# Windowed attention ahead of a mixture of experts: scores issued before the neighbouring unit's transposes, four shared PSUM banks

## The chip, the cores and the metric

The kernel runs on one core of a Trainium2 chip. The core has five engines with queues of their own: TensorE (PE; its weight loads are shown as PEld), VectorE (DVE), ScalarE (ACT), GpSimd (POOL) and SyncE (SP), which here issues the transfers. Matmul results go to PSUM, which has eight banks, each of 512 fp32 per partition. The metric is the device time of one execution in microseconds (us), given as the median of several runs; smaller is better.

## What is computed

Three stages, one after the other: attention with a causal window of 64, a mixture of experts with a greedy assignment under a capacity, and a two-layer network.

```python
B, H, S, D = 4, 8, 576, 64
scores = q @ k.T / 8, kept where 0 <= i - j < 64, otherwise -1e9
attn = exp(scores - rowmax); attn = attn / (attn.sum(-1) + 1e-9)
x = (attn @ v) laid out as [B*S, H*D]            # 2304 tokens of 512
logits = x @ w_gate                              # 8 experts
# greedy: largest logit first, at most 288 tokens per expert, one expert per token
x = relu(x @ w1[e]) @ w2[e]                      # e: the token's expert
h = relu(x @ w_in);  out = (h * h) @ w_out
```

## The kernel before, in words

`attention` comes first and fills some 130 us; then the routing, whose counting needs the logits of all tokens, and the two feed-forward stages follow. Their program is the same in both kernels. The routing starts from the last logits that `attention` writes to `L`.

**Units.** The attention's work is cut into 18 units. Unit 3n+j stands for a batch pair and a block of 64 rows: n (0 to 5) is a pair of batches (n even: batches 0 and 1, n odd: 2 and 3) in a third of the sequence (n//2), j is the block in that third. A unit has two batches times 64 rows on 128 partitions, and eight heads. Four pieces of work belong to a unit:

- `scores(u)`: 32 small matmuls into the tile `sp` (two banks, one buffer; line 130); then eight times on VectorE the mask, scale and row minimum (L135, the tiles t and mn) and on ScalarE the exponential (L136) into P.
- `ptr_(u)`: P is transposed by TensorE in two halves of four transposes (L142), each half into a bank named pt, and each copied to PT by ScalarE (L143).
- `pv(u)`: 32 matmuls of PT with the window of v (L154) into `po` (two banks, one buffer), then on VectorE den (L157), the reciprocal (L159) and X, the product (L160). After the third unit of a pair X is written to DRAM (xs, L163).
- `xtr(u)`: X is transposed for the gate (L169) into a bank pt and copied to XT by VectorE (L172).

Once in three units there are also `logits(n)` (12 small matmuls into a bank pt, L176, and a copy to LT on VectorE, L177) and, a step later, `turn(n)` (one transpose into a bank pt, L180, and a copy to L on VectorE, L181).

**k and q.** `tr(n, h, p)` transposes four heads of k and of q of one batch of the pair: four transposes of kn and four of qn (L110). The result of kn is copied to KT by VectorE (L114), that of qn to QT by ScalarE (L115). A pair n needs four of them before the scores of unit 3n. Before the change kn has a bank of its own (pkn) and qn another (pqn); all else that is transposed, and logits, share the two banks of pt. So the eight banks are pkn 1, pqn 1, pt 2, sp 2, po 2.

**Order.** TensorE's order is written out by hand: a loop over steps s = 0 to 17. The scores of unit 0 go ahead of the loop. Step s issues `ptr_` of unit s-1, the scores of unit s, the transfers that fall due (`pump(s)`), the first `tr` that is due, `xtr` of unit s-2, `pv` of unit s-1, `logits` where s%3 is 2, the other `tr`, and `turn` where s%3 is 0. The `tr` of pair n fall due in the steps 3n-3, 3n-2 (two) and 3n-1, by the list `due`. Where times are given, a step runs from the start of its scores to the start of the next step's. So steps 9, 12 have one `tr` and a `turn`, steps 10, 13 two `tr`, steps 11, 14 one `tr` and `logits`. The instructions on an engine stay in this order; what is due on several engines is tied by semaphores.

**Transfers.** All loads of q, k and v and the writes of xs are issued on SP's queue in the order in which `load_qk`, `load_v` and `pv` are called. A v tile is a window of 128 rows for a unit, of which 64 come by DMA (L64) and the other 64 are copied by GpSimd from the window before (L66). `pump(s)` takes them from a list with due steps. Unit 11's windows fall due in step 6; their copy reads unit 10's windows.

**Constants.** At the end of step 6 the call `between()` issues the routing's constants. On GpSimd these are iotas (L276) and two large memsets (L284, L285), behind unit 11's copies; on VectorE a multiply of the tile `tab` (L282), which needs GpSimd's iota of the same tile, and small memsets.

Of the kernel before, what the change touches and what calls it, by code (L numbers as in the profile page):

```python
# [21 lines left out]
def attention(tc, nc, q,k,v,wgate, xs, L, identf, between=lambda: None, before_last=lambda: None, WARM=(8,4,4,4), NW=14):  # L22


    with ExitStack() as st:
# [71 lines left out]
        nc.sync.dma_start(wg[:,:,0:8], A(wgate,0,[[8,128],[128*8,4],[1,8]]))  # L97
        pump(-1)
        state={}
        def tr(n, h, p):  # L100

            g=n//2
            if n not in QT: QT[n]=wk.tile([128,2,4,T3],F32,name="qt",bufs=2)
            ps_={}
            for nm in ("kn","qn"):
                ps_[nm]=ps.tile([128,2,T3],F32,name="p"+nm,bufs=1)
                for e in range(2):
                    hp=2*p+e
                    for c in range(2):
                        nc.tensor.transpose(ps_[nm][:,e,c*96:c*96+96],N_[nm,n,h][:,c,2*hp:2*hp+2,:].rearrange("p h d -> p (h d)"),identf[:96,:96])  # L110

            def out(t): return t.rearrange("p e (u c) -> p e c u",c=2)
            def inp(t): return t.rearrange("p e (c u) -> p e c u",c=2)
            nc.vector.tensor_copy(out(KT[:,batch(n,h),2*p:2*p+2,g*T3:(g+1)*T3]),inp(ps_["kn"]))  # L114
            nc.scalar.copy(out(QT[n][:,h,2*p:2*p+2]),inp(ps_["qn"]))  # L115
        def scores(u, hps=range(4), sp=None):

            n,j=u
            i=block(u)
            s0=64*max(i-1,0)  # L120
            if sp is None:
                sp=ps.tile([128,2,4,128],F32,name="sp",bufs=1)
                sp=[sp[:,r] for r in range(2)]
            if u not in state: state[u]=wk.tile([128,2,4,128],F32,name="P",bufs=2)
            P=state[u]
            for hp in hps:
                for r in range(2):
                    a=slice(64*r,64*r+64)
                    for h in range(2):
                        nc.tensor.matmul(sp[r][64*h:64*h+64,hp,:],QT[n][a,h,hp,64*j:64*j+64],KT[a,batch(n,h),hp,s0:s0+128],start=True,stop=True)  # L130
            for r in range(2):
                t=wk.tile([128,4,128],F32,name="t",bufs=3)
                mn=wk.tile([128,4],F32,name="mn",bufs=3)
                for hp in hps:
                    nc.vector.tensor_tensor_reduce(out=t[:,hp,:],in0=sp[r][:,hp,:],in1=MK[:,int(i>0)].rearrange("p a b -> p (a b)"),scale=-0.125,scalar=3.0e38,op0=OP.add,op1=OP.min,accum_out=mn[:,hp:hp+1])  # L135
                    nc.scalar.activation(P[:,r,hp,:],t[:,hp,:],AF.Exp,scale=-1.0,bias=mn[:,hp:hp+1])  # L136
        def ptr_(u):
            P=state[u]
            PT=wk.tile([128,2,4,128],F32,name="PT")
            for r in range(2):  # L140
                pt=ps.tile([128,4,128],F32,name="pt",bufs=2)
                for hp in range(4): nc.tensor.transpose(pt[:,hp,:],P[:,r,hp,:],identf)  # L142
                nc.scalar.copy(PT[:,r],pt)  # L143
            state[u]=PT
# [20 lines left out]
        XT={}  # L165
        def xtr(u):
            n,j=u
            xp=ps.tile([128,4,128],F32,name="pt",bufs=2)
            for hp in range(4): nc.tensor.transpose(xp[:,hp,:],X[n][:,j,hp].rearrange("p r d -> p (r d)"),identf)  # L169
            XT[u]=wk.tile([128,4,128],F32,name="XT",bufs=4)  # L170
            if u==units[-1]: nc.scalar.copy(XT[u],xp)
            else: nc.vector.tensor_copy(XT[u],xp)  # L172
        def logits(n):
            lp=ps.tile([128,512],F32,name="pt",bufs=2)
            for hp in range(4):
                for j in range(3): nc.tensor.matmul(lp[32*j:32*j+32,0:128],wg[:,hp],XT[n,j][:,hp],start=hp==0,stop=hp==3)  # L176
            nc.vector.tensor_copy(LT,lp[0:96,0:128])  # L177
        def turn(n):
            lt=ps.tile([128,512],F32,name="pt",bufs=2)[:,0:96]
            nc.tensor.transpose(lt,LT,identf[:96,:96])  # L180
            nc.vector.tensor_copy(L[:,3*n:3*n+3,:],lt.rearrange("p (j e) -> p j e",e=32)[:,:,0:8])  # L181
        def logits_at_once(u, out):
# [5 lines left out]
        for p in range(2):  # L188
            for h in range(2):
                keep_warm(WARM[2*p+h])  # L190
                tr(0,h,p)
            if p==0: scores(units[0],range(0,2),[ps.tile([128,4,128],F32,name="pt",bufs=2) for _ in range(2)])
            else: scores(units[0],range(2,4))
        due={}
        for n in range(1,6):
            for x,z in zip(((0,0),(1,0),(0,1),(1,1)),(0,1,1,2)): due.setdefault(3*n-3+z,[]).append((n,*x))
        for s in range(N):
            if s>0:
                ptr_(units[s-1])
                scores(units[s])  # L200
            pump(s)
            for x in due.get(s,[])[:1]: tr(*x)
            if s>1: xtr(units[s-2])
            if s>0: pv(units[s-1])
            if s>4 and s%3==2: logits(s//3-1)
            for x in due.get(s,[])[1:]: tr(*x)
            if s>5 and s%3==0: turn(s//3-2)
            if s==6: between()
        lt=ps.tile([128,2,4,128],F32,name="sp",bufs=1)[:,0,0]
# [822 lines left out]
```

## Time and profile before

| | us |
|---|---|
| median of 3 runs | 864.88 (859.79 to 866.14) |
| the profiled execution | 867.07 |
| its span, first to last instruction | 865.4 |
| TensorE busy in it | 789.8 (91%) |
| VectorE, ScalarE, GpSimd busy | 467.8, 402.5, 271.5 |
| mean granted TensorE clock | 0.953 of full speed |

Times in the profile count from the start of the span. The profiled execution is a single one; the median is over other runs. The attention's last matmuls stand at about 132 us.

### The profile page before, as it was taken

Reading aid. Unit: us, or ns where it says so; the run is one execution under the profiler, and the core shown is the slowest. Engines: PE = TensorE matmul, PEld = TensorE weight load, DVE = VectorE, ACT = ScalarE, POOL = GpSimd, SP = SyncE. Lnnn points to the kernel's source line nnn. Section 1 sums busy time; section 2 is a strip of 40 time slices with the busy share of each in tenths; the row PEclk is TensorE's granted clock in tenths of the full one; section 3 lists DMA queues with packets and bytes.
Section 4 is the critical chain, followed back from the end, with each engine's and each line's share of the span. In section 5 each row is a group of like instructions: output and inputs, shape, how many; then the busy total and the mean of one; then the engine's idle time right before and its main releaser. Section 6 shows DMA issues by size and latency. Waiting matters only on the chain.

```text
span 865.4 us, 16299 instructions
## 1 busy us (share of the span) xinstructions
PE 789.8 (91%) x6389; PEld 710.7 (82%) x6389; DVE 467.8 (54%) x1379; ACT 402.5 (47%) x777; POOL 271.5 (31%) x245
## 2 busy tenths in 40 slices
PE   6978884698899888799999999989999999999996
PEld 5767764697898777688799999878998999999995
DVE  2675757686667899587564656523212743221111
ACT  3766750324355554544344554344445545444432
POOL 1242000535434342621243653112212644212102
PEclk8999995698999899999999999999999999999999
DMA  8999212626646646742446443333222554111001
GB/s 174 190 201 195 52 38 91 170 98 126 144 177 227 211 147 206 177 156 73 78 160 183 165 137 139 53 73 62 65 96 66 165 186 136 60 49 49 1 0 73
DMA packets 95516, 104.89 MB, mean 121 GB/s; under 512 B 62160, under 2 KB 70352, under 8 KB 95440
## 3 DMA queue, kind: packets, MB, share of 16 engines
q1 hardware_dynamic: 92368, 94.41, 37.1%
q0 software_dynamic: 3072, 9.45, 6.9%
q8 instruction: 50, 0.82, 0.4%
q14 instruction: 26, 0.21, 0.1%
HBM read 86.01 MB, written 17.84 MB: 120 GB/s over the span
## 4 chain that ended last, share of the span: by engine, by line
PE 32%; issue 18%; POOL 3%; DMA 1%; DVE 0%; ACT 0%; POOLq 0%
PE acc L955 9%; PE l L936 8%; PE acc L841 7%; PE acc L883 7%; POOL wlo L679 2%; DMA xg<-xs,idx 1%; POOL out_dram L925 1%; PE rt L388 1%; PE acc L790 0%; PE rt L421 0%; PE rt L790 0%; PE rt L505 0%; POOL xg L777 0%; DVE M L445 0%; DVE hlo L945 0%
## 5 line engine op out<-in xcount | busy, mean ns | idle before, releaser
L679 POOL TENSOR_TENSOR wlo<-wr,whi 128x512 fp32r<-128x512 f32 x95 | 148.6, 1581 | 277.0 <-ACT whi L666 255.8
L945 DVE TENSOR_TENSOR hlo<-h,hhi 128x384 fp32r<-128x384 f32 x96 | 57.9, 603 | 159.9 <-ACT hhi L943 159.9
L940 ACT ACTIVATE r<-l 128x384 f32<-128x384 f32 x93 | 45.6, 490 | 202.1 <-PE l L936 202.1
L936 PE MATMUL l<-yhi,whi 128*128 128x384 f32 x372 | 127.2, 342 | 1.0 <-ACT r L940 1.0
L936 PE MATMUL l<-yhi,wlo 128*128 128x384 f32 x372 | 127.8, 343 | 0.0
L936 PE MATMUL l<-ylo,whi 128*128 128x384 f32 x372 | 126.9, 341 | 0.0
L955 PE MATMUL acc<-whi,hlo 128*128 128x512 f32 x288 | 116.9, 406 | 1.1 <-DVE hlo L945 1.1
L955 PE MATMUL acc<-wlo,hhi 128*128 128x512 f32 x288 | 116.1, 403 | 0.0
L955 PE MATMUL acc<-whi,hhi 128*128 128x512 f32 x288 | 114.9, 399 | 0.0
L666 ACT CAST whi<-wr 128x1024 fp32r<-128x1024 f32 x96 | 99.8, 1050 | 29.6 <-DVE oh L374 20.8
L679 DVE TENSOR_TENSOR wlo<-wr,whi 128x512 fp32r<-128x512 f32 x97 | 84.4, 877 | 24.8 <-ACT whi L666 24.8
L679 POOL TENSOR_TENSOR wlo<-wt,whi 128x512 fp32r<-128x512 f32 x32 | 49.0, 1554 | 91.0 <-ACT whi L666 89.4
L936 PEld LDWEIGHTS l<-yhi,whi 128*128 128x128 f32 x372 | 71.0, 191 | 5.9 <-ACT r L940 1.3
L936 PEld LDWEIGHTS l<-ylo,whi 128*128 128x128 f32 x372 | 70.7, 190 | 3.8
L841 PE MATMUL acc<-xhi,wlo 128*128 128x288 f32 x256 | 73.1, 298 | 0.0
L936 PEld LDWEIGHTS l<-yhi,wlo 128*128 128x128 f32 x372 | 70.6, 190 | 1.2 <-issue 1.1
L841 PE MATMUL acc<-xhi,whi 128*128 128x288 f32 x232 | 69.9, 301 | 0.0
L841 PE MATMUL acc<-xlo,whi 128*128 128x288 f32 x232 | 69.5, 300 | 0.0
L883 PE MATMUL acc<-hhi,whi 128*128 128x288 f32 x256 | 67.7, 298 | 0.0
L883 PE MATMUL acc<-hhi,wlo 128*128 128x288 f32 x256 | 66.9, 296 | 0.0
L883 PE MATMUL acc<-hlo,whi 128*128 128x288 f32 x256 | 66.7, 297 | 0.0
L955 PEld LDWEIGHTS acc<-whi,hlo 128*128 128x128 f32 x288 | 55.3, 192 | 12.7 <-DVE hlo L945 1.6
(194 smaller groups left out, 1481.1 us busy)
## 6 DMA issues: line engine op xcount, KB each, us to landing
wr<-in_moe_w_dram SPq DMA_DIRECT2D x32, 1024.0 KB, 5.2
wr<-conv SPq DMA_DIRECT2D x16, 1024.0 KB, 4.9
wr<-in_moe_w_in_dram SPq DMA_DIRECT2D x16, 512.0 KB, 4.4
wr<-in_moe_w_out_dram SPq DMA_DIRECT2D x16, 512.0 KB, 5.2
conv<-wt SPq DMA_DIRECT2D x16, 512.0 KB, 3.4
xs<-X SPq DMA_DIRECT2D x12, 384.0 KB, 4.6
kn<-in_k_dram SPq DMA_DIRECT2D x20, 192.0 KB, 4.5
qn<-in_q_dram SPq DMA_DIRECT2D x20, 192.0 KB, 4.7
```

Source lines behind the costliest of these rows:

```text
L388: nc.tensor.matmul(cnt[:,0:8],G[:,c],oh[:,c],start=c==0,stop=c==W-1)
L666: nc.scalar.copy(hi,src)
L679: (nc.gpsimd if p else nc.vector).tensor_tensor(out=lo[:,s],in0=src[:,s],in1=hi[:,s].bitcast(F32),op=OP.subtract)
L841: nc.tensor.matmul(ps[f][:,:CAP],self.w[n0+kk][a][:,f*128:(f+1)*128],x[b][:,kk],start=c==0,stop=c==11)
L883: nc.tensor.matmul(p[:,:CAP],self.w[n0+4+k//2][a][:,o:o+128],h[k][b][:,:CAP],start=c==0,stop=c==23)
L925: st=nc.gpsimd.indirect_dma_start(out=self.out,out_offset=bass.IndirectOffsetOnAxis(ap=idt[:,t:t+1],axis=0),in_=ot,in_offset=None)
L936: nc.tensor.matmul(p[:,:HN],self.w[n0+f][a][:,kk*128:(kk+1)*128],y[half][b][:,kk],start=c==0,stop=c==11)
L940: nc.scalar.activation(r,p[:,:HN],AF.Relu); at=self.clk.aop(HN)
L945: nc.vector.tensor_tensor(out=h["lo"],in0=h2,in1=h["hi"].bitcast(F32),op=OP.subtract); self.clk.op(HN,t,0)
L955: nc.tensor.matmul(acc[3*half+t],h[b][:,t*128:(t+1)*128],w[a][:,512:1024],start=f==0 and c==0,stop=f==15 and c==2)
```

## The change

Three things change in `attention`, and nothing in the arithmetic. First, all transposes and the logits take their bank from one name, pt, with four buffers (a helper `bank` gives the shape); pkn and pqn are gone. Second, `scores` now issues only the matmuls and returns the rest (`exps`: the VectorE and ScalarE part) as a function. In step s the scores of unit s are issued, then from step 4 on the first `tr` that is due, then `ptr_` of unit s-1, and only then the `exps` of unit s. Third, the other `tr` all stand behind `logits`, in the steps up to 3 the first one too, and the four `tr` of pair 1 fall due in the steps 1, 1, 2, 2 and no longer 0, 1, 1, 2.

```diff
--- before.py
+++ after.py
@@ -97,13 +97,17 @@
         nc.sync.dma_start(wg[:,:,0:8], A(wgate,0,[[8,128],[128*8,4],[1,8]]))
         pump(-1)
         state={}
+        def bank(shape):
+            t=ps.tile([128,512],F32,name="pt",bufs=4)
+            if len(shape)==1: return t[:,0:shape[0]]
+            return t[:,0:shape[0]*shape[1]].rearrange("p (a b) -> p a b",b=shape[1])
         def tr(n, h, p):
 
             g=n//2
             if n not in QT: QT[n]=wk.tile([128,2,4,T3],F32,name="qt",bufs=2)
             ps_={}
             for nm in ("kn","qn"):
-                ps_[nm]=ps.tile([128,2,T3],F32,name="p"+nm,bufs=1)
+                ps_[nm]=bank((2,T3))
                 for e in range(2):
                     hp=2*p+e
                     for c in range(2):
@@ -128,6 +132,9 @@
                     a=slice(64*r,64*r+64)
                     for h in range(2):
                         nc.tensor.matmul(sp[r][64*h:64*h+64,hp,:],QT[n][a,h,hp,64*j:64*j+64],KT[a,batch(n,h),hp,s0:s0+128],start=True,stop=True)
+            return lambda: exps(u,hps,sp,P)
+        def exps(u, hps, sp, P):
+            i=block(u)
             for r in range(2):
                 t=wk.tile([128,4,128],F32,name="t",bufs=3)
                 mn=wk.tile([128,4],F32,name="mn",bufs=3)
@@ -138,7 +145,7 @@
             P=state[u]
             PT=wk.tile([128,2,4,128],F32,name="PT")
             for r in range(2):
-                pt=ps.tile([128,4,128],F32,name="pt",bufs=2)
+                pt=bank((4,128))
                 for hp in range(4): nc.tensor.transpose(pt[:,hp,:],P[:,r,hp,:],identf)
                 nc.scalar.copy(PT[:,r],pt)
             state[u]=PT
@@ -165,18 +172,18 @@
         XT={}
         def xtr(u):
             n,j=u
-            xp=ps.tile([128,4,128],F32,name="pt",bufs=2)
+            xp=bank((4,128))
             for hp in range(4): nc.tensor.transpose(xp[:,hp,:],X[n][:,j,hp].rearrange("p r d -> p (r d)"),identf)
             XT[u]=wk.tile([128,4,128],F32,name="XT",bufs=4)
             if u==units[-1]: nc.scalar.copy(XT[u],xp)
             else: nc.vector.tensor_copy(XT[u],xp)
         def logits(n):
-            lp=ps.tile([128,512],F32,name="pt",bufs=2)
+            lp=bank((128,))
             for hp in range(4):
                 for j in range(3): nc.tensor.matmul(lp[32*j:32*j+32,0:128],wg[:,hp],XT[n,j][:,hp],start=hp==0,stop=hp==3)
             nc.vector.tensor_copy(LT,lp[0:96,0:128])
         def turn(n):
-            lt=ps.tile([128,512],F32,name="pt",bufs=2)[:,0:96]
+            lt=bank((96,))
             nc.tensor.transpose(lt,LT,identf[:96,:96])
             nc.vector.tensor_copy(L[:,3*n:3*n+3,:],lt.rearrange("p (j e) -> p j e",e=32)[:,:,0:8])
         def logits_at_once(u, out):
@@ -189,21 +196,25 @@
             for h in range(2):
                 keep_warm(WARM[2*p+h])
                 tr(0,h,p)
-            if p==0: scores(units[0],range(0,2),[ps.tile([128,4,128],F32,name="pt",bufs=2) for _ in range(2)])
-            else: scores(units[0],range(2,4))
+            if p==0: scores(units[0],range(0,2),[bank((4,128)) for _ in range(2)])()
+            else: scores(units[0],range(2,4))()
         due={}
         for n in range(1,6):
-            for x,z in zip(((0,0),(1,0),(0,1),(1,1)),(0,1,1,2)): due.setdefault(3*n-3+z,[]).append((n,*x))
+            for x,z in zip(((0,0),(1,0),(0,1),(1,1)),(1,1,2,2) if n==1 else (0,1,1,2)): due.setdefault(3*n-3+z,[]).append((n,*x))
         for s in range(N):
+            d=due.get(s,[])
             if s>0:
+                then=scores(units[s])
+                if s>3:
+                    for x in d[:1]: tr(*x)
+                    d=d[1:]
                 ptr_(units[s-1])
-                scores(units[s])
+                then()
             pump(s)
-            for x in due.get(s,[])[:1]: tr(*x)
             if s>1: xtr(units[s-2])
             if s>0: pv(units[s-1])
             if s>4 and s%3==2: logits(s//3-1)
-            for x in due.get(s,[])[1:]: tr(*x)
+            for x in d: tr(*x)
             if s>5 and s%3==0: turn(s//3-2)
             if s==6: between()
         lt=ps.tile([128,2,4,128],F32,name="sp",bufs=1)[:,0,0]
```

## Rows read from the trace of the kernel before

The busy times by stretch give, after the stretch and its length, the busy time of TensorE, its weight loads (PEld), VectorE, ScalarE and GpSimd (instructions in brackets), then the granted TensorE clock as a share of 2.4 GHz, the busy share of the DMA engines and GB/s. The rows in order of time give the start, the time from the first instruction's start to the last one's end, engine, line, operation, output<-inputs, shape and count, and in brackets the idle time before and what ended it. The row of waits gives who waited for whom, the total, the number of waits and the longest.

**Rows 1.** Busy time by stretch, steps 11, 12, 13, 15, and 9 to 16.

```profile
84.99:91.27 6.28, 5.60 (x109) 4.60 (x108) 4.01 (x22) 4.24 (x12) 2.40 (x4) 1.00 0.34 75
91.27:97.44 6.17, 4.89 (x86) 3.94 (x86) 3.90 (x22) 4.01 (x11) 0.00 (x0) 1.00 0.06 13
97.44:103.30 5.86, 5.34 (x94) 4.51 (x93) 4.28 (x22) 4.19 (x12) 0.00 (x0) 1.00 0.61 134
109.59:115.29 5.70, 4.22 (x79) 3.27 (x78) 3.44 (x21) 3.62 (x10) 0.00 (x0) 1.00 0.01 3
72.96:119.67 46.71, 39.84 (x725) 32.55 (x724) 30.85 (x173) 31.84 (x88) 3.57 (x6) 1.00 0.44 95
```

**Rows 2.** TensorE in order of time, steps 11 to 13.

```profile
88.35 1.07 PE L176 MATMUL pt<-XT,wg 128*32 128x128 f32 x24
89.36 0.66 PE L142 MATMUL pt<-identf,P 128*128 128x128 f32 x4
...
91.27 1.10 PE L130 MATMUL sp<-kt,qt 64*64 64x128 f32 x32
92.31 0.55 PE L110 MATMUL pkn<-identf,kn 96*128 96x96 f32 x4
...
93.02 0.60 PE L169 MATMUL pt<-identf,X 128*128 128x128 f32 x4
93.56 1.15 PE L154 MATMUL po<-w,PT 128*64 128x65 f32 x32
94.64 0.30 PE L180 MATMUL pt<-identf,lt 96*128 96x96 f32 x1
95.55 0.63 PE L142 MATMUL pt<-identf,P 128*128 128x128 f32 x4 [0.61 <-DVE den L157]
96.85 0.66 PE L142 MATMUL pt<-identf,P 128*128 128x128 f32 x4 [0.68 <-ACT PT L143]
...
102.33 1.04 PE L142 MATMUL pt<-identf,P 128*128 128x128 f32 x8
```

**Rows 3.** VectorE and ScalarE in step 13; TensorE's longest wait, steps 9 to 16.

```profile
98.72 0.29 DVE L135 CUSTOM_DVE_ANT_0 t<-sp,mk 128x128 f32<-128x128 f32 x1 [2.19 <-PE sp L130]
...
99.06 2.45 ACT L136 ACTIVATE P<-t,mn 128x128 f32<-128x128 f32 x8 [0.92 <-DVE mn L135]
...
PE pt L142 <- ACT PT L143: 3.4, 5, 0.7
```

**Rows 4.** SP's queue, GpSimd, VectorE, TensorE in order of time, around step 7.

```profile
49.13 2.89 SPq L64 DMA_DIRECT2D w<-in_v_dram  x2
...
55.51 1.17 POOL L66 COPY w<-w 64x512 f32<-64x512 f32 x2 [3.58 <-DMA w<-in_v_dram]
...
57.08 2.04 POOL L284 MEMSET G<- 128x2304 f16 x1
59.03 2.04 POOL L285 MEMSET A__976<- 128x2304 f16 x1
...
57.19 3.93 DVE L282 TENSOR_SCALAR tab<-tab 128x96 f16<-128x96 f16 x1 [0.34 <-POOL tab L276]
...
60.05 1.15 PE L154 MATMUL po<-w,PT 128*64 128x65 f32 x32
63.23 0.86 PE L110 MATMUL pkn<-identf,kn 96*128 96x96 f32 x4 [2.03 <-DVE kt L114]
...
66.67 1.10 PE L130 MATMUL sp<-kt,qt 64*64 64x128 f32 x32
```

**Rows 5.** Busy time by stretch (columns as in rows 1).

```profile
40.00:50.00 10.00, 9.49 (x186) 8.05 (x176) 7.62 (x43) 7.39 (x22) 2.25 (x4) 1.00 1.15 193
62.00:66.00 4.00, 2.73 (x14) 2.44 (x15) 3.20 (x14) 2.60 (x9) 1.39 (x3) 0.66 0.99 196
```

**Rows 6.** TensorE in order of time, in step 0 and at the end.

```profile
18.14 0.39 PE L110 MATMUL pkn<-identf,kn 96*128 96x96 f32 x1 [4.75 <-DMA kn<-in_k_dram]
...
124.51 0.63 PE L169 MATMUL pt<-identf,X 128*128 128x128 f32 x4 [1.07 <-DVE X L160]
```

## The prediction, made before the changed kernel was run

> **What bounds the kernel now.** The diff touches only the attention, so I read that stage. The busy times by stretch come first: from 72.96 to 119.67 us, which is the whole of steps 9 to 16, TensorE is busy 39.84 of 46.71 us at full clock, VectorE 30.85, ScalarE 31.84, and DMA has little to do [rows 1]. So no engine is full, and a step still takes 6.17, 5.86 or 6.28 us by its place in the group of three. TensorE's order of time shows why: in step 12 its work runs without a gap from 91.27 to about 94.9, then the probability transposes are held 0.61 us before the first half and 0.68 us before the second, and only behind these do the next scores start, at 97.44 [rows 2]. The other two engines wait for these scores: VectorE idles 2.19 us until they are done, and ScalarE's eight exponentials (2.45 us) follow [rows 3]. So the step is a loop: scores, reduce, exponentials, transposes held by a bank or by the exponentials, next scores. The view of waits gives the main hold a name: 3.4 us in 5 waits of 0.7 on PT, the copy that empties the bank of the first half [rows 3]. The second half got the bank that the first had just filled.
>
> One step is different. In step 7 VectorE stands in the multiply of tab from 57.19 for 3.93 us; TensorE, idle 2.03 us behind it, comes to step 8's scores only at 66.67 [rows 4]. That matters below.
>
> **The change, part by part.** *Scores first, four banks.* Nothing is added to the arithmetic; the same matmuls and copies issue in another order. If the scores of unit s go before the transposes of unit s-1, then exponentials and reduce of a unit have nearly a whole step to finish, and TensorE's own work is what is left. From starts in [rows 2]: scores 1.04 (91.27 to 92.31), one tr 0.71 (to 93.02), xtr 0.54 (to 93.56), pv 1.08 (to 94.64), turn 0.30, logits 1.01 (88.35 to 89.36), both halves of ptr_ without a hold 0.97 (102.33 to 103.30). A step with turn then needs 1.04+0.71+0.54+1.08+0.97+0.30 = 4.64; one with two tr 1.04+1.42+0.54+1.08+0.97 = 5.05; one with logits 4.34+1.01 = 5.35. Three steps: 15.04 against 18.31 now (6.17+5.86+6.28).
>
> Does another engine become the bound at that pace? VectorE's work per step is 3.90 to 4.28 and ScalarE's 4.01 to 4.24 [rows 1], under 4.64 to 5.35. ScalarE's chain from the end of one unit's exponentials to the end of the next is its own work, two PT copies, one or two qt copies and 2.45 of exponentials, at most 4.24 and a few handovers. So I take the steps 9 to 14 at TensorE's sum: 2 x 15.04 = 30.08 instead of 36.63 (72.96 to 109.59), a gain of 6.55.
>
> Steps 15 and 16 have no tr left: TensorE needs 3.93 (with turn) and 3.63, but there ScalarE's chain (2.45 + two PT copies + the transposes that wait for the last exponential, about 3.85) is as long. 3.93+3.85 = 7.78 against 10.08 (109.59 to 119.67): 2.30.
>
> *What is late next: step 7.* Steps 1 to 6 get faster too, but I count almost nothing for them. The multiply of tab stands in VectorE's queue behind step 6 and waits for GpSimd's iota. GpSimd reaches it only after the copy of window unit 11 at 55.51, which waits for a v transfer issued at 49.13 [rows 4]. These transfers go through SP's queue in program order, and DMA's share from 40 to 50 us is 1.15 [rows 5], so they queue for DMA too: a quicker TensorE does not bring it sooner. Then the two memsets of GpSimd, 2.04 each, end at 61.07, and the multiply ends at 61.12 [rows 4]. So VectorE is stuck until 61.1 as before; only it gets there about 4 us earlier (step 7 at some 52 us) and waits longer.
>
> Worse, what TensorE can do meanwhile shrinks. In step 7 the kt copy of the tr ahead of ptr_ is behind tab on VectorE. With tr in the shared banks, xtr is the fourth allocation after that tr's kn and needs its bank. Queued behind it: pv, the second tr, the next scores. Before the change, pv was under way from 60.05 [rows 4]. After it they start at about 61.7, after 7 us of idleness. Then TensorE is at the lower clock: after only 2.03 us of idleness the four transposes of kn took 0.86 instead of 0.55 [rows 2, 4], at a mean granted clock of 0.66 from 62 to 66 [rows 5] (1.2 GHz for part of it), and the scores at 66.67 were back at 1.10. So xtr 0.95, pv 2.1 (both as estimates at twice the warm step), tr about 1.2: step 8 starts at 65.9 against 66.67, and step 9 at 65.9+5.35 = 71.25 against 72.96. Gain 1.71. Bounds for this term: if xtr gets a bank that ScalarE empties, xtr, pv and tr are done by 61 and step 8 starts when the reduce of step 7 ends, 63.5, but cold: step 9 about 70.9. If TensorE stays cold for 4 us more, 73.
>
> *The first tr moved.* Step 0 now waits 4.75 us for the k of batch pair 1 with step 1's scores queued behind [rows 6]. Moved to step 1, scores, ptr_ and pv of unit 0 go ahead of that wait, so step 2 starts some 5 us sooner. This is hidden by step 7's wait: I count 0. If that cover were gone it counts (a rival).
>
> *Tail.* The last steps run closer together, and xtr of unit 16, which now starts 4.84 after the scores of step 17 (124.51 against 119.67 [rows 6]), waits for X of the same step's pv. That pv now ends 3.7 after the scores (1.04+0.97+0.54+1.08, and 0.1 for the exponentials); den, reciprocal and X take some 1.6 more (an estimate): 5.3, so 0.46 later. The routing stage starts from there, and I find nothing after it that is tied to absolute time: it moves as a whole.
>
> *New holds.* Four banks are handed out to six or more tiles a step. Between no hold at all and the 0.68 of [rows 3] in each of five steps (3.4), I take 0.9, nearer to none since each tile now has three others between it and its bank's last filling.
>
> Sum: 1.71 + 6.55 + 2.30 - 0.46 - 0.9 = 9.2 us. The profiled execution took 867.07 (span 865.4): 857.9. The median of the runs is 864.88, so 855.7.
>
> By the row, tab took 3.93 us and ended 0.05 after the second memset [rows 4]. The Trainium skill, "SBUF — State Buffer", section "Who interferes with whom", says that VectorE in a two-port mode and GpSimd share a port pair, and that whoever issues first blocks the other wholly. The trace agrees, as far as one case can. By that rule a VectorE that issued first would be through at once, and the time would be that of the third rival below.
>
> **Rivals.**
> *Full gain.* If step 7 does not bind, step 1 ends when the data of batch pair 1 are in: the first lands at 18.14 [rows 6], seven more of 197 kB each (96 rows of 8 heads of 64) follow at 193 GB/s [rows 5], so 25; step 2 takes 5.05 and some 2 more for a low clock, so step 3 starts at 32; steps 3 to 7 take 4.34+5.05+5.35+4.64+5.05 = 24.4: step 8 at 56.5, 9.4 better than above. Gain 18.6: 846.3. For it: TensorE's sums. Against: the transfer issued at 49.13, with DMA full [rows 4, 5].
> *Holds stay.* If second halves again get the bank just filled, five or so holds of 0.68 remain: gain 9.2-(3.4-0.9) = 6.7, and with a hold in steps 9, 15 and 16 too about 5.5: 859. For it: the trace shows that banks are not handed out strictly in turn. Against: four are there to choose from.
> *VectorE gets ahead of the memsets.* If the multiply of tab starts before GpSimd's memsets and not in their midst, VectorE is through at about 57.4 instead of 61.1, and step 8 starts some four earlier: 851.7. For it: the multiply ends when they end. Against it: it started 0.11 after the first one [rows 4], and the same iota would release both again.
> *Slower: two holds in every step.* If ptr_'s second half and then xtr each get the bank filled last, each waits for its copy, 0.7 a time, with everything else queued behind. Three steps take 15.04+4.2 = 19.24 against 18.31; two threes lose 1.9, steps 15 and 16 0.5, the tail 0.5, and step 8 is even: about 3 us slower, 868. It decides from 1.09 us of new holds per step, the gain in (18.31-15.04)/3. For it: one such hold a step in [rows 2]. Against: it needs two.
> *The data come too late.* tr now stands ahead of ptr_ and would hold it. From 85 to 97 us DMA's share is 0.34 and then 0.06 [rows 1], so the last k and q are in before that, while the tr that wants the last of them comes in step 13, at 71.25+15.04+4.64, near 91. No cost unless they come 6 us later than now.
>
> **How the numbers follow.** Forecast 0.57 (853 to 858.5), holds stay 0.22, VectorE ahead 0.07, full gain 0.05, slower 0.09. The range 848.5 to 861.5 leaves out the full gain, most of slower and a little of each end. Faster by over 1% means under 856.2 (1% is about what a measurement of this kernel tells from no change): a bit over half of the forecast's 0.57 (0.33), nearly all of the two better ones (0.12), a little of the holds and of a favourable step 7 (0.06): 0.51. Slower by over 1% (over 873.5): 0.04. The rest, 0.45, within.
>
> **What would show it.** Right: scores start before ptr_ of the unit before; steps 9 to 14 take about 15 us a three, with TensorE over 95% busy; PT's hold is gone from the waits; tab still ends near 61, with TensorE idle for some 7 us ahead of it and a lower clock after; the last step's scores start at about 110. Wrong: steps of 9 to 14 still near 6; holds of 0.7 at ptr_ or xtr; tab early and step 8 in the fifties; the routing stage longer or shorter than before.

## The result, and the profile after

The change is faster. Its median is 850.7 us (849.02 to 852.84, 4 runs) against 863.15 us (859.79 to 866.14, 4 runs) for the kernel before, measured beside it, a ratio of 0.985 with a 95% interval of 0.981 to 0.989. The forecast was 855.7 us, with a range from 848.5 to 861.5: the direction and the range hold, and the gain is 12.5 us instead of 9.2.

The profiled execution took 851.18 us, with a span of 849.5. I compare it stage by stage with the one before (span 865.4). The attention ends where TensorE's first routing matmul (tile rt) starts: at 133.22 us before and at 119.22 after, 14.0 us earlier. From there to the end of the span it is 732.2 us before and 730.3 after; the program there is the same, and the experiments show how much this rest varies by itself.

First the stage that the change was about. Busy times by stretch after the change, steps 9, 10, 11, 14, 15, 16, and step 8 last (columns as in rows 1):

```profile
68.85:73.33 4.48, 4.48 (x89) 3.98 (x86) 3.32 (x21) 3.04 (x9) 0.73 (x3) 1.00 1.09 183
73.33:78.38 5.05, 5.05 (x94) 4.53 (x93) 4.42 (x25) 4.42 (x14) 1.06 (x2) 1.00 1.08 205
78.38:83.65 5.27, 5.27 (x110) 4.66 (x109) 4.51 (x23) 4.46 (x14) 0.60 (x1) 1.00 0.85 217
...
93.17:98.92 5.75, 5.60 (x109) 4.60 (x108) 4.58 (x23) 4.78 (x15) 0.00 (x0) 1.00 0.10 31
98.92:102.74 3.82, 3.82 (x80) 3.31 (x78) 2.95 (x20) 2.46 (x8) 0.00 (x0) 1.00 0.02 4
102.74:106.32 3.58, 3.58 (x77) 3.17 (x76) 3.33 (x21) 3.17 (x11) 0.00 (x0) 1.00 0.35 78
...
61.23:68.85 7.62, 7.62 (x108) 6.85 (x109) 5.71 (x26) 4.86 (x15) 2.32 (x4) 0.67 0.91 218
```

In steps 9 to 11 TensorE's busy time equals the length of the step: 4.48, 5.05 and 5.27 us, where [rows 1] had gaps of 0.5 to 1.3. TensorE in order of time, step 12, answers to [rows 2]:

```profile
83.65 1.10 PE L134 MATMUL sp<-kt,qt 64*64 64x128 f32 x32
84.68 0.55 PE L114 MATMUL pt<-identf,kn 96*128 96x96 f32 x4
85.07 0.49 PE L114 MATMUL pt<-identf,qn 96*128 96x96 f32 x4
85.40 1.04 PE L149 MATMUL pt<-identf,P 128*128 128x128 f32 x8
86.27 0.60 PE L176 MATMUL pt<-identf,X 128*128 128x128 f32 x4
86.80 1.15 PE L161 MATMUL po<-w,PT 128*64 128x65 f32 x32
87.89 0.30 PE L187 MATMUL pt<-identf,lt 96*128 96x96 f32 x1
88.12 1.10 PE L134 MATMUL sp<-kt,qt 64*64 64x128 f32 x32
```

No row carries an idle time in brackets. The probability transposes (L149) run as one group of eight, where [rows 2] had two halves with holds of 0.61 and 0.68. All of TensorE's waits between 25 and 119 us:

```profile
PE sp L134 <- DVE mn L142: 4.6, 1, 4.6
PE sp L190 <- ACT XT L178: 0.7, 1, 0.7
PE pt L176 <- DVE X L167: 0.6, 2, 0.3
PE po L161 <- issue: 0.3, 1, 0.3
PE pt L149 <- ACT qt L119: 0.2, 1, 0.2
```

The hold by PT, the longest of [rows 3], is gone. One large wait is left: 4.6 us once, at the scores of step 8. TensorE in order of time around it:

```profile
53.24 1.04 PE L149 MATMUL pt<-identf,P 128*128 128x128 f32 x8
54.12 0.60 PE L176 MATMUL pt<-identf,X 128*128 128x128 f32 x4
54.65 1.15 PE L161 MATMUL po<-w,PT 128*64 128x65 f32 x32
55.73 0.55 PE L114 MATMUL pt<-identf,kn 96*128 96x96 f32 x4
56.12 0.49 PE L114 MATMUL pt<-identf,qn 96*128 96x96 f32 x4
61.23 1.99 PE L134 MATMUL sp<-kt,qt 64*64 64x128 f32 x32 [4.62 <-DVE mn L142]
63.15 0.90 PE L114 MATMUL pt<-identf,kn 96*128 96x96 f32 x4
63.84 0.84 PE L114 MATMUL pt<-identf,qn 96*128 96x96 f32 x4
64.48 1.91 PE L149 MATMUL pt<-identf,P 128*128 128x128 f32 x8
```

And the engines it waits for, VectorE first, then GpSimd and SP's queue, the answer to [rows 4]:

```profile
55.45 3.93 DVE L293 TENSOR_SCALAR tab<-tab 128x96 f16<-128x96 f16 x1 [2.83 <-POOL tab L287]
55.93 3.46 DVE L118 COPY kt<-pt 128x384 f32<-128x384 f32 x1
```

```profile
53.15 0.61 POOL L66 COPY w<-w 64x512 f32<-64x512 f32 x1 [2.04 <-PE pt L114]
54.34 0.61 POOL L66 COPY w<-w 64x512 f32<-64x512 f32 x1 [0.58 <-PE pt L149]
...
55.35 2.04 POOL L295 MEMSET G<- 128x2304 f16 x1
57.30 2.04 POOL L296 MEMSET A__976<- 128x2304 f16 x1
```

```profile
48.01 2.86 SPq L64 DMA_DIRECT2D w<-in_v_dram  x2
```

What to read here: the two v transfers of the last row are issued at 48.0 and 49.4 and land 5.0 and 4.8 us later, at 53.0 and 54.2. GpSimd's two copies start 0.1 us after each landing, so it is the transfers that they wait for, although the brackets name TensorE. VectorE arrives earlier than before, idles 2.83 us for GpSimd's iota behind these copies, and stands in the multiply of tab beside the memsets until 59.38. The kt copy behind it ends with it. But TensorE does not stop at once, as I had forecast: xtr, pv and the second tr run on (54.12 to 56.6) while kt is stuck. It stops only at the scores, whose two banks (`sp`) hold step 7's scores until VectorE has reduced them. Then it comes back slower: the 32 score matmuls take 1.99 us instead of 1.10, and the stretch of step 8 has a granted clock of 0.67 (2.4 GHz is 1.00, 1.2 GHz 0.50).

### The profile page after: what moved, and what is told of

Same layout as the page of the kernel before. It is cut to its first block, busy times and chain, and to the rows that moved or that the text cites. A ratio compares the mean times of both kernels' runs of the same rounds, so it can differ in the third digit from the quotient of the medians.

```text
span 849.5 us, 16319 instructions
## 1 busy us (share of the span) xinstructions
PE 784.7 (92%) x6389; PEld 710.7 (84%) x6389; DVE 472.0 (56%) x1379; ACT 400.1 (47%) x777; POOL 268.7 (32%) x245
## 3 DMA queue, kind: packets, MB, share of 16 engines
q0 software_dynamic: 3072, 9.45, 7.0%
## 4 chain that ended last, share of the span: by engine, by line
PE 33%; issue 18%; POOL 3%; DMA 1%; DVE 0%; ACT 0%; POOLq 0%
PE acc L966 9%; PE l L947 8%; PE acc L852 8%; PE acc L894 7%; POOL wlo L690 2%; DMA xg<-xs,idx 1%; POOL out_dram L936 1%; PE rt L399 0%; PE acc L801 0%; PE rt L801 0%; PE rt L516 0%; DVE M L456 0%; PE rt L432 0%; DVE hlo L956 0%; POOLq L690 0%
## 5 line engine op out<-in xcount | busy, mean ns | idle before, releaser
L947 PEld LDWEIGHTS l<-yhi,whi 128*128 128x128 f32 x372 | 70.9, 191 | 5.0 <-ACT r L951 0.6
L690 POOL TENSOR_TENSOR wlo<-wt,whi 128x512 fp32r<-128x512 f32 x32 | 45.6, 1451 | 90.1 <-ACT whi L677 88.5
```

Source lines behind the costliest of these rows:

```text
L690: (nc.gpsimd if p else nc.vector).tensor_tensor(out=lo[:,s],in0=src[:,s],in1=hi[:,s].bitcast(F32),op=OP.subtract)
L947: nc.tensor.matmul(p[:,:HN],self.w[n0+f][a][:,kk*128:(kk+1)*128],y[half][b][:,kk],start=c==0,stop=c==11)
```

## The experiments

The theory after the result: the loop of [rows 2] is broken and TensorE's own sum is what is left; step 7's wait for tab is the one large price that remains; xtr escaped because it got a bank that ScalarE had emptied; the first tr, moved later, is hidden. The rivals: one part of the change carries it alone, the banks or the order; the memsets aren't what holds VectorE; the rest of the program answers to the change.

Each ratio is against the kernel before on the same chip, whose median was 863.15 us for the change, 863.82 for the next four rows, 870.3 for the four behind them and 863.96 for the last four; so medians are compared within these groups only. Times within the span are of one profiled execution each, in us.

| kernel | step 8 | step 9 | steps 9 to 14 | first routing matmul | median | ratio (95%) |
|---|---|---|---|---|---|---|
| before | 66.67 | 72.96 | 36.63 | 133.22 | see above | 1 |
| the change | 61.23 | 68.85 | 30.07 | 119.22 | 850.7 | 0.985 (0.981 to 0.989) |
| banks only | 65.28 | 71.40 | 31.99 | 124.92 | 851.66 | 0.985 (0.982 to 0.989) |
| order only | 62.91 | 71.42 | 32.38 | 126.38 | 858.35 | 0.992 (0.989 to 0.996) |
| strict rotation | 64.64 | 69.89 | 29.53 | 120.27 | 853.2 | 0.987 (0.983 to 0.991) |
| constants early | 57.46 | 63.22 | 30.56 | 114.86 | 845.45 | 0.979 (0.975 to 0.983) |
| first tr back | 62.88 | 70.29 | 30.06 | 120.66 | 856.6 | 0.987 (0.982 to 0.992) |
| before, constants early | 63.99 | 70.05 | 36.61 | 129.61 | 865.31 | 0.997 (0.994 to 0.999) |
| memsets apart | 59.67 | 67.71 | 30.07 | 118.88 | 854.23 | 0.983 (0.977 to 0.990) |
| early and rotation | 57.71 | 62.95 | 29.54 | 112.87 | 846.94 | 0.975 (0.970 to 0.980) |
| the change again | 61.29 | 68.74 | 30.08 | 119.12 | 852.36 | 0.987 (0.984 to 0.990) |
| banks only again | 66.09 | 71.90 | 32.00 | 125.43 | 855.79 | 0.992 (0.989 to 0.995) |
| constants early again | 56.48 | 62.24 | 30.56 | 113.11 | 846.04 | 0.978 (0.974 to 0.981) |
| early and rotation again | 56.85 | 62.09 | 29.53 | 112.22 | 844.17 | 0.976 (0.973 to 0.979) |

**Banks only.** The order of before, with all transposes in the four shared banks (part of the edit; the due steps of pair 1 are as before too).

```diff
             if s>0:
-                then=scores(units[s])
-                if s>3:
-                    for x in d[:1]: tr(*x)
-                    d=d[1:]
                 ptr_(units[s-1])
-                then()
+                scores(units[s])
             pump(s)
+            for x in due.get(s,[])[:1]: tr(*x)
```

> The four shared banks alone, in the order of before. Theory 'either is enough': with no bank to wait for, the old loop (scores 1.04, reduce and exponentials until 4.05 after the start of the scores, second half of ptr_, next scores) closes after about 4.85 us, which is under or near TensorE's own sum, so steps 9 to 14 take 30.5 to 31.5 us (36.63 before, 30.07 after) and the time is 853 to 856. Rival 'the order carries it': the banks only take away the holds named in the trace of before (about 3.4 us on PT, 1 on qt and den), steps 9 to 14 take 32.5 or more and the time is 858 or more.

Steps 9 to 14 took 31.99 us. Of the 6.56 that the change gains there, the banks alone gain 4.64. TensorE's waits from 71.4 to 112 us:

```profile
PE pt L146 <- ACT qt L119: 0.9, 4, 0.3
```

With four banks the hold by PT is gone without any change of order; ScalarE's copy of qt takes its place, at 0.2 to 0.3 a time. The six steps lie between my 30.5 to 31.5 and the rival's 32.5. In step 7 this kernel still stops: the q transposes of the second `tr` wait 4.47 us for a bank until the kt copy has ended, and step 8 starts at 65.28. The ratio was no different from the change's and the median, 851.66, was under my 853 to 856, though the attention ended 5.7 us later (124.92): the rest took 724.7 us in this profile, 5.6 less than in that of the change. That called for the repetition below.

**Order only.** The order of the change, with the banks of before (pkn 1, pqn 1, pt 2).

```diff
-            t=ps.tile([128,512],F32,name="pt",bufs=4)
+            t=ps.tile([128,512],F32,name="pt",bufs=2)
...
-                ps_[nm]=bank((2,T3))
+                ps_[nm]=ps.tile([128,2,T3],F32,name="p"+nm,bufs=1)
```

> The new order alone, with one bank each for kn and qn and two for the rest as before. Theory 'either is enough': the copies have time, only xtr can be held behind the copy of the first half of ptr_, 0.2 to 0.3 us a step; steps 9 to 14 take 31 to 32 us and the time is 852 to 855. Rival 'the banks carry it': the hold of 0.68 behind PT stays once or twice a step, steps 9 to 14 take 34 us or more and the time is 857 or more.

Steps 9 to 14 took 32.38, a gain of 4.25, and TensorE's waits from 71.4 to 112 us are these:

```profile
PE pt L176 <- ACT PT L150: 2.0, 8, 0.3
```

With two banks, xtr (L176) behind the two halves of `ptr_` needs a bank that one of them has just filled, once in each of the eight steps, for 0.25 us. So either part alone gives about two thirds, and both together 6.56 and not 8.89 (4.64 + 4.25): for the most part they remove the same hold. Neither rival stands. What each part leaves, the other takes away. Between my 31 to 32 and the rival's 34, the steps are nearer to mine; the total, 858.35, is in the rival's 857 or more and not in my 852 to 855.

**Strict rotation.** Four names of one buffer each, handed out in turn.

```diff
-        state={}
+        state={}; turns=[0]
...
-            t=ps.tile([128,512],F32,name="pt",bufs=4)
+            t=ps.tile([128,512],F32,name=f"pt{turns[0]%4}",bufs=1); turns[0]+=1
```

> The changed kernel with its four banks handed out strictly in turn. If my step on step 7 failed because xtr of step 7 got a bank that ScalarE had emptied, then now it gets that of the k transposes, whose copy stands behind tab on VectorE: TensorE stops ahead of xtr at about 54.1 until the kt copy ends at about 59.4, and step 8's scores start at 63 to 64 instead of 61.23; steps 9 to 14 stay at 30.1; the time is 1.5 to 2.5 us above the changed kernel's, some 852.5 to 853. Rival: the bank plays no part there, step 8 at 61.2 and no difference.

This makes the stop that I had predicted for the change. TensorE in order of time, step 7, and VectorE's multiply:

```profile
53.87 1.04 PE L149 MATMUL pt<-identf,P 128*128 128x128 f32 x8
60.57 1.12 PE L176 MATMUL pt<-identf,X 128*128 128x128 f32 x4 [5.66 <-DVE kt L118]
61.62 2.00 PE L161 MATMUL po<-w,PT 128*64 128x65 f32 x32
63.55 0.83 PE L114 MATMUL pt<-identf,kn 96*128 96x96 f32 x4
64.22 0.49 PE L114 MATMUL pt<-identf,qn 96*128 96x96 f32 x4
64.64 1.10 PE L134 MATMUL sp<-kt,qt 64*64 64x128 f32 x32
...
56.51 3.93 DVE L293 TENSOR_SCALAR tab<-tab 128x96 f16<-128x96 f16 x1 [3.25 <-POOL tab L287]
```

In turn, xtr does need kn's bank and waits 5.66 us for its copy; step 8 starts at 64.64, 3.4 later than in the change. Of that, 1.06 is a later tab: it ends at 60.44 here and at 59.38 in the change. Counted from the end of tab, step 8 starts 4.20 us later here and 1.85 in the change, but step 9 starts 9.45 later here and 9.47 in the change. So by step 9 the stop has cost nothing. Here the slow stretch (a granted clock of 0.56 from 60.57 to 64.64) lies ahead of step 8, which then takes 5.25 us; in the change it lies in step 8, which takes 7.62. The median, 853.2, and the ratio, 0.987, can't be told from the change's ratio of 0.985. In the steady steps rotation is the better: 29.53 us for steps 9 to 14, not the 30.1 that I expected, with no hold at all. That is TensorE's own sum. The change's 30.07 holds some 0.5 more, in step 14, where the second half of `ptr_` waits for the qt copy.

**Constants early.** The routing's constants (the iotas, tab, the memsets) move from the end of step 6 to the start of the program, ahead of the window copies.

```diff
         for t in W_: nc.vector.memset(t[:,:,64:66],1.0)
+        between()
...
-            if s==6: between()
```

> The changed kernel with the routing's constants issued ahead of the window copies at the start of the program instead of after step 6. Theory 'step 7's wait is the price of tab': no wait in step 7, step 8's scores at 56.6 instead of 61.23, no fall of the clock there, step 17's scores at 99 to 100 instead of 106.3; the first kt copy comes some 2 us later, hidden behind the k of pair 1; the time is 843 to 845. Rival 'the transfers bind next': k and q of pairs 4 and 5, issued as before, hold TensorE in steps 9 to 13, and only 2 to 4 us are won: 847 to 849.

The wait of 4.6 us is gone, steps 7 and 8 run at full clock, and the attention ends 4.4 us earlier than in the change, 18.4 earlier than before. Step 8 starts at 57.46, against 56.5 for the rival "full gain" of the prediction, and the median is 845.45 against its 846.3. So step 7's wait is what keeps the change from that rival. (I had expected step 8 at 56.6 and 843 to 845, a little better.) All of TensorE's waits from 24 to 101 us in this kernel:

```profile
PE pt L115 <- DMA qn<-in_q_dram: 0.6, 1, 0.6
PE pt L150 <- ACT qt L120: 0.5, 3, 0.2
```

The second line costs more than its 0.5: the steps 8, 11 and 14 take 5.76 each, against 5.24 in the strict rotation, for the transposes then run as two halves with a bank handed over between them. So step 17 starts at 101.18 and not at 99 to 100.

**Memsets apart.** Constants stay where they are, but the two large memsets are issued after step 12.

```diff
-        self.G=t([128,18,128],F16,"G"); g.memset(self.G,0.0)
-        self.A_=t([128,18,128],F16,"A_"); g.memset(self.A_,0.0)
+        self.G=t([128,18,128],F16,"G")
+        self.A_=t([128,18,128],F16,"A_")
...
+    def zeros(self):
+        self.nc.gpsimd.memset(self.G,0.0); self.nc.gpsimd.memset(self.A_,0.0)
...
             if s==6: between()
+            if s==12: zeros()
```

> The changed kernel, constants after step 6 as they are, but GpSimd's two large memsets issued after step 12. Theory 'two waits, one behind the other': VectorE still waits some 2.8 us for the iota, until about 55.5, but tab then takes 0.2 us or less instead of 3.93, the kt copy ends near 56, step 8's scores start at 57.5 to 58 instead of 61.23, TensorE is idle about 1 us instead of 4.6 and its clock stays up; the time is 845.5 to 847.5. Rival 'the iota is the wait': tab short, but something else (the copies behind it, the clock) keeps step 8 after 60, 849 or more.

VectorE in order of time:

```profile
56.91 0.19 DVE L294 TENSOR_SCALAR tab<-tab 128x96 f16<-128x96 f16 x1 [4.85 <-POOL tab L288]
...
57.38 0.55 DVE L118 COPY kt<-pt 128x384 f32<-128x384 f32 x1
```

The multiply takes 0.19 us instead of 3.93, the kt copy 0.55 instead of 3.46: the memsets hold VectorE, that much is shown. The Trainium skill, "SBUF — State Buffer", section "Who interferes with whom", says that VectorE in a two-port mode and GpSimd take one shared port pair, and that the one that issues second is blocked completely. The trace agrees, as far as times can: 0.19 us without the memsets, 3.93 behind them, in every profile where the first memset started about 0.1 us before. In one point it shows more: in the change the multiply, started at 55.45, waited for the second memset too, which started at 57.30. No view shows the mode that the multiply ran in. My number for the step missed: 59.67 instead of 57.5 to 58. The scores of step 8 start 2.8 us after the iota has ended (56.87 to 59.67), where the change needs 5.8 (55.42 to 61.23): 3.0 saved. But the iota itself came 1.45 later in this run, and an idle time of 3.62 us was left, enough for the scores to take 1.99 again. So the wait for the v transfer is enough to open the gap; the memsets lengthen it. The total tells no gain: step 9 starts 1.1 us earlier than in the change, but the attention ends only 0.3 earlier (118.88), since the last eight gate matmuls took 1.85 us instead of 1.06, and the ratio of 0.983 (0.977 to 0.990) can't be told from the change's.

**First tr back.** The four tr of pair 1 fall due at 0, 1, 1, 2 again.

```diff
-            for x,z in zip(((0,0),(1,0),(0,1),(1,1)),(1,1,2,2) if n==1 else (0,1,1,2)): due.setdefault(3*n-3+z,[]).append((n,*x))
+            for x,z in zip(((0,0),(1,0),(0,1),(1,1)),(0,1,1,2)): due.setdefault(3*n-3+z,[]).append((n,*x))
```

> The changed kernel with the four tr of pair 1 due in the steps 0, 1, 1, 2 again, as before the change. Theory 'hidden by step 7's wait': step 1's scores wait behind the k of pair 1 and come at 21 to 23 instead of 14.3, step 2's some 2 us late, but tab on VectorE still ends near 59 to 60, step 8's scores stay within 0.5 us of 61.2 and the time is that of the changed kernel (850 to 852.5). Rival 'the moved tr is worth its wait': step 8 comes 2 us or more later, 853 or more.

Step 1 starts at 21.09 instead of 14.33, step 2 at 28.20 instead of 25.16, step 7 only at 52.57 instead of 51.49, and step 8 starts 1.85 us after the multiply of tab ends (61.03), as in the change (59.38 and 61.23). With or without the move, step 8 starts from tab. The tab ended 1.65 us later than in the change, and so step 8, at 62.88, lies between my 0.5 us and the rival's 2. That need not be the edit's: the memsets-apart kernel, run on the same chip with the new due steps, had its iota nearly as late (56.87, and 57.07 here). The ratios, 0.987 and 0.985, can't be told apart. So no worth of the move is shown here, as I had counted; whether it counts once tab is out of the way was not run.

**Before, constants early.** The same move of the constants in the kernel before.

```diff
         for t in W_: nc.vector.memset(t[:,:,64:66],1.0)
+        between()
...
-            if s==6: between()
```

> The kernel before, with the routing's constants at the start of the program. Theory 'tab costs the old order less, since it gets there later': step 7 takes 5.9 instead of 8.90 us, step 8's scores come 3 us earlier than 66.67, the other steps stay, the time is about 3 us less than before: 860 to 861.5. In the changed kernel the same edit brought 4.4 us up to the first routing matmul. Rival: the wait is worth as much here (4.4 us or more), 859 or less.

Step 7 takes 5.85 us instead of 8.90, and the attention ends 3.6 us earlier; the total falls by 0.3% (0.1 to 0.6%), about what 3.6 us would give. So the wait cost the kernel before as well: 3.6 us there, 4.4 in the change. (The 860 to 861.5 that I expected can't be set against the median of 865.31, since the kernel before took 870.3 in this group.)

**Early and rotation.** Constants early together with strict rotation.

```diff
+        between()
...
-        state={}
+        state={}; turns=[0]
...
-            t=ps.tile([128,512],F32,name="pt",bufs=4)
+            t=ps.tile([128,512],F32,name=f"pt{turns[0]%4}",bufs=1); turns[0]+=1
...
-            if s==6: between()
```

> The changed kernel with the constants at the start and the four banks strictly in turn. Theory 'rotation only hurts where VectorE stands still': with no such place left it only takes away the hold of some 0.5 us that the second half of ptr_ has in the steps 8, 11 and 14 of the kernel with early constants alone; steps 9 to 14 take 29.5 us instead of 30.56, the first routing matmul comes at 113 to 113.5 instead of 114.86, the time is 843.5 to 844.5. Rival: some other bank is late once VectorE is never waited for, steps 9 to 14 at 30.5 or more, 845.5 or more.

With the stop of step 7 gone, rotation costs nothing there and keeps its even steps. TensorE's waits from 24 to 101 us:

```profile
PE pt L115 <- DMA qn<-in_q_dram: 0.9, 2, 0.6
```

Not one hold by a bank is left.

**The four that matter, again, on one chip.** Since the rest of the program had differed so much between profiles, the change, banks only, constants early, and early with rotation ran side by side.

> The changed kernel once more, beside the three below on one chip, since the runs so far were on several chips and what follows the attention took between 724.7 and 732.2 us in profiles of one and the same program. Ratio to the kernel before as measured, 0.981 to 0.989; first routing matmul at 119 to 121.

> Four shared banks in the old order, again. Its attention ended 5.7 us later than the changed kernel's, its time was the same. Theory 'what follows varies by itself': on the same chip its median is 3 to 7 us above the changed kernel's (ratio to before 0.988 to 0.993), with the first routing matmul near 125 again. Rival 'the rest of the program gains when the attention ends as it does there': the medians are within 1.5 us again, with the rest some 5 us shorter in the profile again.

> The changed kernel with the constants at the start, again: first routing matmul at 114.9, 4.4 us ahead of the changed kernel. Theory: its median is 3.5 to 6 us under the changed kernel's. Rival (the rest eats it): under 2.

> Constants at the start and strict rotation, again: first routing matmul at 112.9, 6.3 us ahead of the changed kernel. Theory: its median is 5 to 8 us under the changed kernel's and 1 to 3 under that of early constants alone. Rival: no difference to early constants alone that can be measured.

Medians: 852.36 (850.17 to 854.11), 855.79 (853.57 to 861.43), 846.04 (839.49 to 846.42), 844.17 (840.72 to 846.84). The order is now that in which the attention ends (119.12, 125.43, 113.11, 112.22). Banks only is 3.4 us above the change, so its equal ratio of the first time was a matter of the rest. The best version, constants early with strict rotation, beats both kernels: 8.2 us under the change and 19.8 under before (863.96). Its step over constants early alone, 1.9 us, lies within the spread of the runs; within the attention it is 0.9 to 2.0 us (113.11 to 112.22 and 114.86 to 112.87).

The rest, from the first routing matmul to the end, took 724.7 and 728.0 us in the two profiles of banks only, 725.9 and 731.6 in those of constants early, 730.3 and 731.8 in those of the change. The same program thus differs by up to 5.7 us between executions. TensorE's clock goes with it. The rest in the two profiles of banks only, then in those of constants early (columns as in rows 1):

```profile
124.92:849.60 724.68, 673.36 (x4640) 613.49 (x4639) 387.67 (x955) 325.71 (x570) 248.28 (x192) 0.96 0.39 119
...
125.43:853.40 727.97, 679.77 (x4640) 619.30 (x4639) 387.49 (x955) 325.52 (x570) 245.29 (x192) 0.95 0.39 118
...
114.86:840.80 725.94, 676.80 (x4640) 616.40 (x4639) 386.65 (x955) 325.39 (x570) 245.49 (x192) 0.96 0.39 118
...
113.11:844.70 731.59, 680.36 (x4640) 619.91 (x4639) 390.04 (x955) 325.70 (x570) 244.09 (x192) 0.95 0.39 118
```

The two profiles of a pair are from different chips. In both pairs the shorter rest has the higher granted clock (0.96 and 0.95), and the same 4640 matmuls keep TensorE busy for 6.4 and 3.6 us less. In the two profiles of the change it is the same in small: 679.06 busy of 730.28 and 681.14 of 731.78. What sets the clock in the rest is open.

## Why the prediction was right or wrong

**The loop: right.** Scores ahead of `ptr_` and four banks leave TensorE's sum. I forecast 30.08 us for steps 9 to 14 and they took 30.07. That the two agree to 0.01 is luck: without any hold the six steps take 29.53 (strict rotation), so the sum was 0.55 too long (the steps with turn and with logits take 4.47 and 5.24, not 4.64 and 5.35; both halves of `ptr_` take 0.87 from start to start, not 0.97), and some 0.5 of holds is in the measured value. That VectorE and ScalarE would not become the bound was right: 4.6 and 4.8 us at most, in a step of 5.75.

**Steps 15 and 16: right, a little short.** 7.40 against 7.78 forecast, 10.08 before. ScalarE's chain, which I had at 3.85 us for step 16, held nothing: the two steps took 3.82 and 3.58, and TensorE was busy for all of them.

**New holds: mis-sized.** 0.9 us was forecast; the waits show 0.15 of idle time, in step 14, which is 0.5 longer for it. The rival "holds stay" (859) and the slower one (two holds a step) both fall. Order only shows what the second needed: with two banks xtr did wait behind `ptr_` in each step, though for 0.25 us and not 0.7.

**Step 7: the step that failed.** "With tr in the shared banks, xtr is the fourth allocation after that tr's kn and needs its bank." The premise was that banks are handed out in turn, although the prediction itself quoted the trace that they are not. In the change xtr got a bank that was already empty, shown by its start at 54.12 with kt stuck until 59.39; strict rotation, where the premise does hold, gave the stop that I had priced. My bound for this term named the case ("if xtr gets a bank that ScalarE empties", step 9 at about 70.9), and that is what came, with tab 1.7 us earlier. In time, though, the wrong premise cost next to nothing. Step 9 starts 9.47 us after the end of tab in the change and 9.45 in strict rotation; the forecast had 10.15 (61.1 to 71.25). The bank changed where TensorE stood still, not when step 9 began.

**tab "stuck until 61.1 as before": wrong by 1.7.** It ended at 59.38. The order of cause was right (transfer, copy, iota, memsets, multiply), but the v transfers were issued at 48.0 and 49.4 and not at 49.1 and 50.4, and the second landed at 54.2 and not at 55.8. In the runs of the change and of its parts tab started anywhere from 55.45 to 57.24, and in memsets apart, the same program up to there, at 56.91; so whether the change brought it forward or the executions differ is not shown, and this part of the gain may be luck. Step 8 came at 61.23 where I had 65.9: 1.7 us by the earlier tab, 2.35 by xtr's freedom (1.85 instead of 4.20 after tab), and 0.6 because I had priced the stop too high. The lower clock, which I had placed ahead of step 8, then fell on step 8, 7.62 us instead of 5.35, and took xtr's part back. Step 9 started at 68.85: a gain of 4.11 against 1.71 forecast. Of the 2.40 between them, 1.7 is tab and 0.7 the price of the stop and the slow work; 0.5 of this is the kt copy, which I let run after tab and which ends with it.

**The moved tr: right as to its price.** No worth of it is shown; it is hidden behind tab. But of the 5 us by which step 2 was to come sooner, 3.0 came (25.16 instead of 28.20), and 1.1 were left at step 7.

**The tail: right mechanism, wrong size and sign.** TensorE's last eight gate matmuls, before and after:

```profile
131.30 1.65 PE L183 MATMUL sp<-wg,XT 128*128 128x8 f32 x8 [0.68 <-ACT XT L171]
...
117.89 1.06 PE L190 MATMUL sp<-wg,XT 128*128 128x8 f32 x8 [0.68 <-ACT XT L178]
```

In the change, xtr of unit 16 starts 4.97 us after the last step's scores (5.3 forecast, 4.84 before), so 0.13 is lost there. But the last eight gate matmuls ran at full clock (1.06 us; before, 1.65 at a granted clock of 0.57 from 131.3 to 133.2). From the last scores to the routing it is 12.90 us against 13.55, a gain of 0.65 instead of a loss of 0.46. It is not shown that this gain comes from the change: in the two profiles of constants early the same eight took 1.84 us (a granted clock of 0.52) and 1.06.

**The sum.** 4.11 + 6.56 + 2.68 + 0.65 = 14.0 us up to the routing, against 9.2 forecast. The difference of 4.8 is step 9 (2.40), the tail (1.11), the holds (0.9) and steps 15 and 16 (0.38). So more than half of it, tab's 1.7 and the tail's 1.11, hangs on things that were seen to differ between executions.

**"It moves as a whole": not quite.** In the profiles the rest became 1.9 us shorter, but in the medians only 12.5 of the 14.0 us arrive, and 11.6 in the last group of runs. The profiled execution of before, at 867.07 us, was longer than all the runs in its median, so the profiled pair overstates the difference. That a part of the gain is given back in the routing or the networks is possible; with a rest that varies by 5.7 us these runs can't show it.

## What to carry to other kernels

When a step is a loop through several engines with a bank in it, breaking it at the bank or in the order of issue removes largely the same hold (here 4.64 and 4.25 us alone, 6.56 together): try each alone before adding their gains. When a bank is suspected, compare a step behind the slow stretch and not the stop itself: the stop of 5.66 us in strict rotation no longer told at step 9. Then look for a wait that is tied to a transfer and not to the loop (here transfer, copy, iota, memsets, multiply): it eats whatever the steps before it gain, and moving the constants out of its way was worth another 4 to 6 us. Judge such a change in its own stage of the profile, where 0.1 us can be read, and take the total from several runs on one chip, since the untouched rest can vary by more than the part in question; TensorE's granted clock in the rest tells whether it did.

## What the runs showed of the hardware

- Two GpSimd memsets of 2.04 us make a multiply of 128x96 fp16 on VectorE last 3.93 us instead of 0.19, and the copy queued behind it, which reads PSUM, shows 3.46 instead of 0.55. The memset was ahead by about 0.1 us in every profile in which both followed the same iota, at the start of the kernel too (4.27 and 4.39 in constants early). The multiply ended with the second memset, not with the first.
- After idle times of 4.62 (the change), 3.62 (memsets apart) and 2.03 us (before) TensorE's next work ran slower: scores 1.99 us instead of 1.10 after the first two, the transposes of kn 0.86 instead of 0.55 after the third [rows 2, 4]. The granted clock was 0.67 and 0.63 in step 8 of the first two and 0.66 from 62 to 66 us in the third [rows 5]. In the change it cost step 8 some 2.35 us (7.62 against 5.27 in step 11).
- Not of the chip, but of how the program's buffers are handed out: buffers of one name are not taken in turn. In one and the same program order, xtr went ahead at once when they came from one name with four buffers, and waited 5.66 us when they went round.
